# Batch 0 of a cosformer attention: k's sums by a selector weight, an earlier k^T v, and fewer idle matmuls

## The chip, the cores and the metric

The kernel runs on one core of a Trainium2 chip. The metric is the device time of one launch in microseconds (us). A core has five engines that run their own instruction queues in order and meet through semaphores: TensorE (matmuls and weight loads; PE and PEld in the profile), VectorE (DVE), ScalarE (ACT), GpSimd (POOL) and SyncE (SP), the last two also issuing DMAs. A matmul reads its two operands from SBUF and writes PSUM; VectorE and ScalarE carry PSUM back to SBUF.

## The reference

```python
def phi(x, c, s):                       # c, s: cos and sin of pi/2 * position / S
    r = np.maximum(x, 0.0)
    return np.concatenate([r * c, r * s], axis=-1)
q_p, k_p = phi(q, cos_w, sin_w), phi(k, cos_w, sin_w)
kv  = np.einsum('bhsf,bhsd->bhfd', k_p, v)
z   = np.sum(k_p, axis=2)
num = np.einsum('bhsf,bhfd->bhsd', q_p, kv)
den = np.einsum('bhsf,bhf->bhs', q_p, z)[..., None] + 1e-06
attn = num / den                        # 8 batches, 8 heads, S = 576, head size 64
x = attn.transpose(0, 2, 1, 3).reshape(B * S, H * D)          # 4608 x 512
h = x @ w_in                            # 512 -> 2048
g = h * (1.0 / (1.0 + np.exp(-1.702 * h)))
out = g @ w_out                         # 2048 -> 512
```

q, k, v, the weights and the output are float32; the matmuls run in bfloat16.

## The kernel before, in words

The sequence of a batch is cut into nine slots j of 64 rows. Two heads (hh) lie on the two halves of the 128 partitions, and four such pairs (i) side by side. For batch 0, k, q and v are loaded in this layout (`kf`, `qf0`, `vb`), k and q by SyncE in two pieces each (L62, L63), v as bfloat16 by GpSimd in two halves of two pairs (L130).

`trig` (L138 to L145) makes phi of one slot: two instructions, one with the cosine and one with the sine as a scale per partition, on VectorE or with `act=True` on ScalarE. It fills `kr` from k and `qn0` from q. `kv_mm` (L205 on) accumulates k^T v in PSUM for pairs i0 to i1 with `kr` as the stationary operand, a half of the partitions at a time; with a column of ones in place of v the same function gives k's sums, as column 64 beside the 64 of k^T v. `kv_evac` (L213) casts the result into `kvs`, from which later matmuls read 65 columns. `qturn_pe(c)` transposes q's slots 2c and 2c+1 on TensorE, `qevac(c)` carries them from PSUM into `qT`. `num_mm(c)` multiplies 128 rows of q with `kvs`, numerator and denominator in one (L223); `num_div(c)` divides on VectorE into `xn` (L231 to L235). `xturn_mm` (L253) and `xturn_evac` (L260, ScalarE) transpose xn into `xT`, which the first layer reads (`mm1_part`, L276). `start_block` interleaves the last of these with the first layer's first four column blocks of 128.

The order of work is written out by hand and each engine keeps it. PSUM tiles come from two pools: four buffers "mm" of one bank, two buffers "at" of two banks. `idle(n)` (L335) issues n matmuls of 512 columns on a tile of zeros, whose results nobody reads. The program starts with 23 of them, while k and q come in.

On GpSimd's queue stand, in this order: a small copy that waits for k's first piece (L128), v's halves for batch 0, two blocks of w_in (`load_win`, L122), a small copy that waits for v's second half (L133), the other two blocks of w_in, and then the loads of batch 1 and of w_out.

After batch 0's attention TensorE runs the two layers of one batch after the other, with the next batch's attention woven in; nothing of that is touched.

Of the kernel before, what the change touches and what calls it, by code (L numbers as in the profile page):

```python
# [9 lines left out]
F32 = mybir.dt.float32  # L10
BF16 = mybir.dt.bfloat16
AF = mybir.ActivationFunctionType
MUL = mybir.AluOpType.mult
ADD = mybir.AluOpType.add
MAX = mybir.AluOpType.max
# [4 lines left out]
def kernel(  # L20
# [9 lines left out]
    nc = tc.nc  # L30
# [5 lines left out]
    NS = S // 64  # L36
    MT = 512
    NI = H // 2

    const = ctx.enter_context(tc.tile_pool(name="const", bufs=1))  # L40
# [4 lines left out]
    small = ctx.enter_context(tc.tile_pool(name="small", bufs=3))  # L45
    pmm = ctx.enter_context(tc.tile_pool(name="pmm", bufs=4, space=PSUM))
# [5 lines left out]
    def raw(name, dt=F32):  # L52
        return one.tile([128, NI, S], dt, name=name)
# [5 lines left out]
    kf, vf, vb = raw("kf"), raw("vf"), raw("vb", BF16)  # L59
    qf0 = qf[:, 0:NI * S].rearrange("p (i e) -> p i e", i=NI)  # L60
    for t, src, cut in ((kf, k, 192), (qf0, q, 256)):
# [9 lines left out]
    ident = const.tile([128, 128], BF16)  # L71
# [3 lines left out]
    warm = const.tile([128, 512], BF16)  # L75
# [6 lines left out]
    scale = math.pi / 2.0 / S  # L82
    halfpi = const.tile([128, 1], F32)
    nc.vector.memset(halfpi, math.pi / 2.0)
    ones = const.tile([128, 2], BF16)
    nc.vector.memset(ones, 1.0)
    nc.scalar.activation(sinw, pos_f, AF.Sin, scale=scale)
    nc.scalar.activation(cosw, pos_f, AF.Sin, scale=-scale, bias=halfpi)
    gl = const.tile([128, 1], F32)
# [3 lines left out]
    kr = one.tile([128, NS, NI, 128], BF16, name="kr")  # L93
    vt = one.tile([128, NS, NI, VW], BF16, name="vt")
    qn = one.tile([128, 5, H, 128], BF16, name="qn")
    qn0 = qn.rearrange("p c h f -> p (c h f)")[:, 0:NS * NI * 128].rearrange(
        "p (j i f) -> p j i f", j=NS, i=NI)
# [23 lines left out]
    def load_win(g):  # L121
        nc.gpsimd.dma_start(out=w_in_sb[g], in_=win_r[:, :, ts(g, 512)])  # L122
# [4 lines left out]
    gate = const.tile([1, 4], F32)  # L127
# [2 lines left out]
        nc.gpsimd.dma_start(out=vb[:, i:i + 2], in_=src_of(v, 0, i, i + 2))  # L130
    load_win(0)
    load_win(1)
    nc.gpsimd.tensor_copy(gate[0:1, 1:2], vb[0:1, 3, 0:1])  # L133
    load_win(2)
    load_win(3)


    def trig(dst, src, j, act=False):  # L138
        i = src[:, :, ts(j, 64)]
        for cs, w in enumerate((cosw, sinw)):  # L140
            o = dst[:, j, :, ts(cs, 64)]
            if act:
                nc.scalar.activation(o, i, AF.Relu, scale=w[:, j:j + 1])
            else:
                nc.vector.tensor_scalar(o, i, 0.0, w[:, j:j + 1], op0=MAX, op1=MUL)  # L145

    def trig_q(c, act=False):
        n = 128 if c < 4 else 64
# [21 lines left out]
    def qturn_pe(c, home=None):  # L170
        tp = pmm.tile([128, 2, NI, 128], BF16, name="mm") if home is None else home
        for j in range(2 * c, min(2 * c + 2, NS)):
            for i in range(NI):
                nc.tensor.transpose(tp[:, j % 2, i], qn0[:, j, i, :], ident)  # L174
        tps[c] = tp

    def qevac(c, act=False):
        n = min(2 * c + 2, NS) - 2 * c
        o = qT[:, :, ds(c * 128, n * 64)].rearrange("f h (j p) -> f j h p", j=n)
        i = tps.pop(c)[:, 0:n].rearrange("f j i (hh p) -> f j (i hh) p", hh=2)  # L180
        if act:
            nc.scalar.activation(o, i, AF.Copy)
        else:
            nc.vector.tensor_copy(o, i)
# [10 lines left out]
    st = {}  # L195

    def kv_open(i0=0, i1=NI):
        t = pat.tile([128, 2, 512], F32, name="at")
        for i in range(i0, i1):
            st["kv", i] = t[:, :, ds((i - i0) * 65, 65)]  # L200
        st["ps", i0] = t[:, :, 0:(i1 - i0) * 65]
        if i0 == 0:
            st["kvs"] = small.tile([128, 2, NI, VW], BF16, name="kvs", bufs=2)

    def kv_mm(i0, i1, rhs, col, n):  # L205
        for i in range(i0, i1):
            for j in range(NS):
                for hh in range(2):
                    r = slice(hh * 64, hh * 64 + 64)
                    nc.tensor.matmul(st["kv", i][:, hh, ds(col, n)], kr[r, j, i, :], rhs(r, i, j),  # L210
                                     start=(j == 0), stop=(j == NS - 1))

    def kv_evac(i0, i1):  # L213
        o = st["kvs"][:, :, i0:i1, 0:65]
        nc.vector.tensor_copy(o, st["ps", i0].rearrange("p hh (i e) -> p hh i e", e=65))  # L215

    nums = {}

    def num_mm(c):
        ps = pat.tile([128, 2, 512], F32, name="at")  # L220
        for h in range(H):
            i, hh = divmod(h, 2)
            nc.tensor.matmul(ps[:, h // 4, ds((h % 4) * 65, 65)], qT[:, h, ts(c, 128)],  # L223
                             st["kvs"][:, hh, i, 0:65], start=True, stop=True)
        nums[c] = [ps]

    def num_div(c):
        ps = nums[c][0]
        pv = ps[:, :, 0:260].rearrange("p a (h e) -> p a h e", h=4)
        den = small.tile([128, 2, 4], F32, name="den")  # L230
        nc.vector.tensor_scalar(den, pv[:, :, :, 64], 1e-6, None, op0=ADD)  # L231
        inv = small.tile([128, 2, 4], F32, name="inv")
        nc.vector.reciprocal(inv, den)
        xn = small.tile([128, 2, 4, 64], BF16, name="xn", bufs=4)
        nc.vector.tensor_tensor(xn, pv[:, :, :, 0:64],  # L235
                                inv.unsqueeze(3).to_broadcast([128, 2, 4, 64]), op=MUL)
        nums[c].append(xn)
# [7 lines left out]
    def x_open(b):  # L245
        x[b] = xpool.tile([128, KC, S], BF16, name="xT")
# [85 lines left out]
                eng = nc.sync if b == B - 1 else nc.gpsimd  # L332
                eng.dma_start(out=dst[:, c0:c1], in_=ysb[p0:p0 + n, c0:c1])  # L333

    def idle(n, cols=512):  # L335
        w = pmm.tile([128, 512], F32, name="mm")
        for _ in range(n):
            nc.tensor.matmul(w[:, 0:cols], warm[:, 0:128], warm[:, 0:cols], start=True, stop=True)  # L338

    def vb_rhs(r, i, j):  # L340
        return vb[r, i, ts(j, 64)]
# [4 lines left out]
    def start_block(b, opened=False):  # L346

        if not opened:
            xturn_mm(0)
            xturn_evac(b, 0)  # L350
            num_mm(2)
            num_div(2)
            xturn_mm(1)
            xturn_evac(b, 1)
        for c in range(4):
            for fc in range(4):
                mm1_part(b, fc, c * 128, c * 128 + 128)
            if c == 0:
                num_mm(3)
                num_div(3)  # L360
                xturn_mm(2)
                xturn_evac(b, 2)
            if c == 1:
                num_mm(4)
                num_div(4)
                xturn_mm(3)
                xturn_evac(b, 3)
        for fc in range(4):
            gelu(fc)
        mm1(b, 4)  # L370
        xturn_mm(4)
        xturn_evac(b, 4)


    idle(23)
    for j in (0, 1):
        trig(kr, kf, j)
    for j in (2, 6, 7, 8):
        trig(kr, kf, j, act=True)
    for j in (3, 4, 5):  # L380
        trig(kr, kf, j)
    kv_open(0, 2)
    kv_open(2, 4)
    kv_mm(0, NI, lambda r, i, j: ones[r, 0:1], 64, 1)
    for j in (0, 1):
        trig(qn0, qf0, j)
    qturn_pe(0)
    for j in (2, 3):
        trig(qn0, qf0, j, act=True)
    qturn_pe(1)  # L390
    idle(3)
    for j in (4, 5):
        trig(qn0, qf0, j)
    qturn_pe(2)
    for j in (6, 7):
        trig(qn0, qf0, j, act=True)
    qevac(0)
    trig(qn0, qf0, 8)
    qevac(1)
    qevac(2, act=True)  # L400
    kv_mm(0, 2, vb_rhs, 0, 64)
    qturn_pe(3)
    qevac(3, act=True)
    kv_evac(0, 2)
    qturn_pe(4)
    qevac(4)
    kv_mm(2, 4, vb_rhs, 0, 64)
    kv_evac(2, 4)
    num_mm(0)
    num_div(0)  # L410
    num_mm(1)
    num_div(1)
    x_open(0)
    start_block(0)

# [44 lines left out]
    kv_open()  # L460
    kv_mm(0, 4, vt_rhs, 0, 65)
    kv_evac(0, 4)
    mm2(0, 2, 8, 12)
    mm2(0, 3, 8, 12)
# [96 lines left out]
```

## Time and profile before

| | us |
|---|---|
| three runs | 294.86, 296.48, 297.08 |
| median | 296.48 |
| the profiled execution's own time | 296.72 |
| its span, first to last instruction | 295.0 |
| TensorE busy | 288.4 (98%) |
| VectorE, ScalarE, GpSimd busy | 126.7, 130.7, 34.7 |

The span is what the rows of the profile cover; the time of the execution is a little longer. A row of the timeline gives start and duration of a run of like instructions, and in brackets how long the engine stood idle before it and what released it. Matmuls are pipelined, so the duration of one is longer than the distance to the next. The granted clock is the share of TensorE's full clock that its throttle let through. Over the whole span its mean is 0.994.

### The profile page before, as it was taken

How to read it: one execution, taken by the hardware profiler on the slowest of the kernel's cores; microseconds unless marked ns; L12 is line 12 of the kernel's file. 1: busy time of each engine (PE TensorE's matmuls, PEld its weight loads, DVE VectorE, ACT ScalarE, POOL GpSimd, SP SyncE). 2: the span in 40 equal slices, each digit the busy share in tenths (PEclk: the TensorE clock that was granted, in tenths of full speed). 3: DMA queues.
4: the chain of work that ended last, by engine and by line, in shares of the span. 5: the costliest groups of instructions: out<-in, count | busy, mean ns of one | idle time of the engine just before them, and what ended most of it. 6: DMA issues, size and time to landing. Idle time of an engine off the chain costs nothing.

```text
span 295.0 us, 6106 instructions
## 1 busy us (share of the span) xinstructions
PE 288.4 (98%) x2498; PEld 161.7 (55%) x2498; DVE 126.7 (43%) x363; ACT 130.7 (44%) x229; POOL 34.7 (12%) x68
## 2 busy tenths in 40 slices
PE   8979999999999999999999999999999999999995
PEld 2776656757454555455545554555455545565444
DVE  4855513693255825671567156454752420000000
ACT  7827653676014631374126412651166017773111
POOL 6340031500123001100110011000100010000000
PEclk9979999999999999999999999999999999999999
DMA  7999969667168974698569936996595240000321
GB/s 251 240 220 288 368 143 379 196 130 194 36 122 239 315 192 121 195 337 214 90 195 354 224 94 150 321 188 194 138 384 112 71 116 37 1 0 3 86 90 71
DMA packets 67227, 52.36 MB, mean 177 GB/s; under 512 B 47392, under 2 KB 57376, under 8 KB 67200
## 3 DMA queue, kind: packets, MB, share of 16 engines
q1 hardware_dynamic: 59824, 32.52, 42.8%
q0 software_dynamic: 7376, 19.47, 23.2%
q8 instruction: 19, 0.31, 0.4%
q14 instruction: 8, 0.07, 0.1%
HBM read 36.70 MB, written 9.44 MB: 156 GB/s over the span
## 4 chain that ended last, share of the span: by engine, by line
PE 98%; DVE 1%; ACT 0%; issue 0%; ACTq 0%
PE mm L326 42%; PE mm L276 38%; PE at L210 4%; PE mm L294 4%; PE at L223 3%; PE mm L338 3%; PE mm L303 1%; PE at L253 1%; PE mm L174 1%; PE at L174 1%; DVE xn L235 0%; ACT xT L260 0%; DVE kvs L215 0%; ACT ysb L330 0%; DVE warm L76 0%
## 5 line engine op out<-in xcount | busy, mean ns | idle before, releaser
L326 PE MATMUL mm<-w_out_sb,g 128*128 128x512 bf16 (+1 forms) x528 | 117.7, 373 | 0.0
L276 PE MATMUL mm<-xT,w_in 128*128 128x512 bf16 (+1 forms) x608 | 114.4, 348 | 0.0
L281 ACT ACTIVATE g<-mm 128x512 bf16<-128x512 f32 x128 | 75.6, 598 | 31.9 <-PE mm L276 31.9
L276 PEld LDWEIGHTS <-w_in 128*128 128x128 bf16 x608 | 62.7, 115 | 49.0
L326 PEld LDWEIGHTS <-g 128*128 128x128 bf16 x528 | 48.7, 98 | 49.5
L330 ACT ACTIVATE ysb<-mm 128x512 f32<-128x512 f32 (+1 forms) x37 | 21.7, 586 | 111.4 <-PE mm L326 111.4
L333 POOL DMA_DIRECT2D out_dram<-ysb x38 | 20.7, 548 | 177.3 <-ACT ysb L330 177.2
L145 DVE TENSOR_SCALAR kr<-kf,cosw 128x256 bf16<-128x256 f32 x68 | 23.6, 348 | 27.8 <-DMA kf<-in_k_dram 27.8
L235 DVE TENSOR_TENSOR xn<-at,inv 128x512 bf16<-128x512 f32 x40 | 27.6, 691 | 1.4
L145 DVE TENSOR_SCALAR kr<-kf,sinw 128x256 bf16<-128x256 f32 x68 | 23.8, 350 | 0.0
L231 DVE TENSOR_SCALAR den<-at 128x8 f32<-128x8 f32 x40 | 6.6, 166 | 38.6 <-PE at L223 38.6
L223 PEld LDWEIGHTS <-qT 128*128 128x128 bf16 x320 | 15.0, 99 | 8.6 <-issue 1.2
L215 DVE CAST kvs<-at 128x520 bf16<-128x520 f32 (+1 forms) x9 | 5.8, 642 | 29.8 <-PE at L210 29.8
L223 PE MATMUL at<-kvs,qT 128*128 128x65 bf16 x320 | 16.5, 195 | 1.0 <-ACT xT L260 0.7
L158 DVE TENSOR_SCALAR qn<-qf,sinw 128x512 bf16<-128x512 f32 (+1 forms) x30 | 14.3, 477 | 0.0
L158 DVE TENSOR_SCALAR qn<-qf,cosw 128x512 bf16<-128x512 f32 (+1 forms) x30 | 14.3, 477 | 0.0
L210 PEld LDWEIGHTS <-kr 64*128 64x128 bf16 x648 | 10.2, 94 | 2.8 <-issue 2.0
L294 PE MATMUL mm<-xt,w_in 128*128 128x384 bf16 x64 | 10.6, 326 | 0.0
L326 PE MATMUL mm<-w_out_sb,gl_t 128*128 128x512 bf16 x48 | 10.5, 379 | 0.0
L338 PE MATMUL mm<-warm 128*128 128x512 bf16 x26 | 8.6, 502 | 1.3 <-DVE warm L76 1.3
L294 PEld LDWEIGHTS <-w_in 128*128 128x128 bf16 x64 | 7.2, 113 | 3.3
L260 ACT ACTIVATE xT<-at 128x512 bf16<-128x512 bf16 (+1 forms) x10 | 5.6, 562 | 7.7 <-PE at L253 6.6
(60 smaller groups left out, 123.5 us busy)
## 6 DMA issues: line engine op xcount, KB each, us to landing
kf<-in_k_dram SPq DMA_DIRECT2D x5, 1152.0 KB, 6.7
vf<-in_v_dram SPq DMA_DIRECT2D x5, 1152.0 KB, 9.5
qf<-in_q_dram SPq DMA_DIRECT2D x5, 1024.0 KB, 6.2
out_dram<-ysb POOLq DMA_DIRECT2D x20, 256.0 KB, 3.1
kf<-in_k_dram POOLq DMA_DIRECT2D x2, 1152.0 KB, 10.2
vf<-in_v_dram POOLq DMA_DIRECT2D x2, 1152.0 KB, 14.8
out_dram<-ysb POOLq DMA_DIRECT2D x18, 128.0 KB, 2.7
w_in<-in_moe_w_in_dram POOLq DMA_DIRECT2D x4, 512.0 KB, 10.0
```

The source lines that it names most:

```text
L145: nc.vector.tensor_scalar(o, i, 0.0, w[:, j:j + 1], op0=MAX, op1=MUL)
L158: nc.vector.tensor_scalar(o, i, 0.0, sc, op0=MAX, op1=MUL)
L210: nc.tensor.matmul(st["kv", i][:, hh, ds(col, n)], kr[r, j, i, :], rhs(r, i, j), start=(j == 0), stop=(j == NS - 1))
L223: nc.tensor.matmul(ps[:, h // 4, ds((h % 4) * 65, 65)], qT[:, h, ts(c, 128)], st["kvs"][:, hh, i, 0:65], start=True, stop=True)
L235: nc.vector.tensor_tensor(xn, pv[:, :, :, 0:64], inv.unsqueeze(3).to_broadcast([128, 2, 4, 64]), op=MUL)
L276: nc.tensor.matmul(hp[fc][:, t0:t1], w_in_of(kc, fc), x[b][:, kc, t0:t1], start=(kc == 0), stop=(kc == KC - 1))
L281: nc.scalar.activation(g, hp.pop(fc), AF.Gelu_apprx_sigmoid)
L294: nc.tensor.matmul(hps, w_in_of(kc, fc), xt[:, kc, :], start=(kc == 0), stop=(kc == KC - 1))
L326: nc.tensor.matmul(yp[t, c0][:, c0:c1], w, w_out_sb[:, fc, c0:c1], start=(fc == 0), stop=(fc == FC - 1))
L330: nc.scalar.activation(ysb[:, c0:c1], yp[t, c0][:, c0:c1], AF.Identity)
L333: eng.dma_start(out=dst[:, c0:c1], in_=ysb[p0:p0 + n, c0:c1])
L338: nc.tensor.matmul(w[:, 0:cols], warm[:, 0:128], warm[:, 0:cols], start=True, stop=True)
```

## The change

All of it is in batch 0, ahead of the first layer's first matmul.

- The ones become a selector `sel` of two columns: column hh is 1 on head hh's half of the partitions and 0 elsewhere. `ksum(j)` takes it as the stationary operand and a whole slot of `kr` (512 columns) as the moving one, so nine matmuls replace 72 and give the sums as two rows of 512 in a "mm" buffer. VectorE copies these rows to SBUF (`zr`), `ksum_turn` turns them back with four small transposes, and VectorE puts them into column 64 of `kvs`. `kv_evac` of batch 0 now takes 64 columns.
- The leading idle matmuls are 12 instead of 23. One stands ahead of the ninth sum, one ahead of q's first transposes, and two instead of three behind these. Four more stand between `num_mm(1)` and the first transposes of x. `idle` can go on in a buffer that it has.
- q's slot 8 is rotated on GpSimd instead of VectorE, between w_in's second block and the copy that waits for v.
- The first half of k^T v now stands right behind the transposes of the sums and ahead of q's slots 6 and 7; the second half comes ahead of slot 8's transposes instead of behind them. The evacuation of slots 2 and 3 follows on VectorE behind that of the sums, and slot 8's evacuation goes to ScalarE.

```diff
-    ones = const.tile([128, 2], BF16)
-    nc.vector.memset(ones, 1.0)
+    sel = const.tile([128, 2], BF16)
+    nc.vector.memset(sel, 0.0)
+    for hh in range(2):
+        nc.vector.memset(sel[hh * 64:hh * 64 + 64, hh:hh + 1], 1.0)
...
     load_win(0)
     load_win(1)
-    nc.gpsimd.tensor_copy(gate[0:1, 1:2], vb[0:1, 3, 0:1])
-    load_win(2)
-    load_win(3)
...
+    def ksum(j):
+        if j == 0:
+            st["z"] = pmm.tile([128, 512], F32, name="mm")
+        nc.tensor.matmul(st["z"][0:2], sel, kr[:, j].rearrange("p i f -> p (i f)"),
+                         start=(j == 0), stop=(j == NS - 1))
+
+    def ksum_turn():
+        zt = pmm.tile([128, NI, 2], BF16, name="mm")
+        for i in range(NI):
+            nc.tensor.transpose(zt[:, i], st["zr"][:, ts(i, 128)], ident[0:2, 0:2])
+        nc.vector.tensor_copy(st["kvs"][:, :, :, 64], zt.rearrange("f i hh -> f hh i"))
...
-    idle(23)
+    w = idle(12)
...
     kv_open(0, 2)
     kv_open(2, 4)
-    kv_mm(0, NI, lambda r, i, j: ones[r, 0:1], 64, 1)
+    for j in (0, 1, 2, 3, 6, 4, 7, 5):
+        ksum(j)
+    idle(1, w)
+    ksum(8)
     for j in (0, 1):
         trig(qn0, qf0, j)
+    st["zr"] = small.tile([2, 512], BF16, name="zr", bufs=1)
+    nc.vector.tensor_copy(st["zr"], st["z"][0:2])
+    idle(1, w)
     qturn_pe(0)
     for j in (2, 3):
         trig(qn0, qf0, j, act=True)
+    idle(2, w)
     qturn_pe(1)
-    idle(3)
     for j in (4, 5):
         trig(qn0, qf0, j)
+    trig(qn0, qf0, 8, eng=nc.gpsimd)
+    nc.gpsimd.tensor_copy(gate[0:1, 1:2], vb[0:1, 3, 0:1])
+    load_win(2)
+    load_win(3)
     qturn_pe(2)
     for j in (6, 7):
         trig(qn0, qf0, j, act=True)
     qevac(0)
-    trig(qn0, qf0, 8)
-    qevac(1)
+    ksum_turn()
     qevac(2, act=True)
     kv_mm(0, 2, vb_rhs, 0, 64)
+    qevac(1)
+    kv_evac(0, 2, 64)
     qturn_pe(3)
     qevac(3, act=True)
-    kv_evac(0, 2)
+    kv_mm(2, 4, vb_rhs, 0, 64)
+    kv_evac(2, 4, 64)
     qturn_pe(4)
-    qevac(4)
-    kv_mm(2, 4, vb_rhs, 0, 64)
-    kv_evac(2, 4)
+    qevac(4, act=True)
     num_mm(0)
     num_div(0)
     num_mm(1)
     num_div(1)
+    idle(4)
     x_open(0)
     start_block(0)
```

More of the change, by code (lines that the diff above doesn't have):

```diff
@@ L132, with trig @@
     load_win(1)
-    nc.gpsimd.tensor_copy(gate[0:1, 1:2], vb[0:1, 3, 0:1])
-    load_win(2)
-    load_win(3)
-    def trig(dst, src, j, act=False):
+    def trig(dst, src, j, act=False, eng=nc.vector):
         i = src[:, :, ts(j, 64)]
@@ L144, in trig @@
             else:
-                nc.vector.tensor_scalar(o, i, 0.0, w[:, j:j + 1], op0=MAX, op1=MUL)
+                eng.tensor_scalar(o, i, 0.0, w[:, j:j + 1], op0=MAX, op1=MUL)
     def trig_q(c, act=False):
@@ L211, in kv_mm, with kv_evac @@
                                      start=(j == 0), stop=(j == NS - 1))
-    def kv_evac(i0, i1):
-        o = st["kvs"][:, :, i0:i1, 0:65]
-        nc.vector.tensor_copy(o, st["ps", i0].rearrange("p hh (i e) -> p hh i e", e=65))
+    def kv_evac(i0, i1, n=65):
+        o = st["kvs"][:, :, i0:i1, 0:n]
+        nc.vector.tensor_copy(o, st["ps", i0].rearrange("p hh (i e) -> p hh i e", e=65)[:, :, :, 0:n])
+    def ksum(j):
[8 more added lines that the diff above has]
+        nc.vector.tensor_copy(st["kvs"][:, :, :, 64], zt.rearrange("f i hh -> f hh i"))
     nums = {}
@@ L333, in mm2, with idle @@
                 eng.dma_start(out=dst[:, c0:c1], in_=ysb[p0:p0 + n, c0:c1])
-    def idle(n, cols=512):
-        w = pmm.tile([128, 512], F32, name="mm")
+    def idle(n, w=None):
+        if w is None:
+            w = pmm.tile([128, 512], F32, name="mm")
         for _ in range(n):
-            nc.tensor.matmul(w[:, 0:cols], warm[:, 0:128], warm[:, 0:cols], start=True, stop=True)
+            nc.tensor.matmul(w, warm[:, 0:128], warm, start=True, stop=True)
+        return w
     def vb_rhs(r, i, j):
```

## The prediction

> **What bounds the kernel now.** I read the page's shares first, then the two big matmul groups, then TensorE's timeline.
>
> ```profile
> PE 288.4 (98%) x2498; PEld 161.7 (55%) x2498; DVE 126.7 (43%) x363; ACT 130.7 (44%) x229; POOL 34.7 (12%) x68
> ...
> L326 PE MATMUL mm<-w_out_sb,g 128*128 128x512 bf16 (+1 forms) x528 | 117.7, 373 | 0.0
> L276 PE MATMUL mm<-xT,w_in 128*128 128x512 bf16 (+1 forms) x608 | 114.4, 348 | 0.0
> ```
>
> TensorE is busy in 98% of the span, and its two large groups stood idle for 0.0 us. What comes after batch 0's attention therefore cannot shrink; it can only begin earlier. The edits all lie ahead of it, so the question is when the dense stream begins. Here is TensorE up to that point (start, duration, what; where rows overlap I take start to start):
>
> ```profile
> 1.26 7.84 PE L338 MATMUL mm<-warm 128*128 128x512 bf16 x23 [1.26 <-DVE warm L76]
> 9.03 1.05 PE L210 MATMUL at<-ones,kr 64*128 64x1 bf16 x72
> 10.01 1.07 PE L174 MATMUL mm<-ident,qn 128*128 128x128 bf16 x16
> 10.91 0.81 PE L338 MATMUL mm<-warm 128*128 128x512 bf16 x3
> 11.56 0.61 PE L174 MATMUL mm<-ident,qn 128*128 128x128 bf16 x8
> 12.11 0.71 PE L210 MATMUL at<-vb,kr 64*128 64x64 bf16 x36
> 12.74 0.84 PE L174 MATMUL mm<-ident,qn 128*128 128x128 bf16 x12
> 13.52 0.71 PE L210 MATMUL at<-vb,kr 64*128 64x64 bf16 x36
> ...
> 14.75 0.52 PE L223 MATMUL at<-kvs,qT 128*128 128x65 bf16 x12 [0.30 <-DVE kvs L215]
> 16.26 0.40 PE L253 MATMUL at<-ident,xn 128*128 128x128 bf16 x4 [0.98 <-DVE xn L235]
> 17.34 0.60 PE L223 MATMUL at<-kvs,qT 128*128 128x65 bf16 x8 [0.69 <-ACT xT L260]
> ...
> 18.16 1.91 PE L276 MATMUL mm<-xT,w_in 128*128 128x128 bf16 x16
> 19.87 0.65 PE L223 MATMUL at<-kvs,qT 128*128 128x65 bf16 x8
> ...
> 20.58 1.06 PE L276 MATMUL mm<-xT,w_in 128*128 128x128 bf16 x16
> 21.48 0.41 PE L223 MATMUL at<-kvs,qT 128*128 128x65 bf16 x8
> ...
> 21.97 2.99 PE L276 MATMUL mm<-xT,w_in 128*128 128x128 bf16 x36
> ```
>
> The 21.97 row, where the third column block of the first layer starts, is my marker: whatever moves it moves the end. Two marks stand ahead of it. N, 14.75, is the second half of num_mm(0), released by the cast of k^T v. S, 17.34, is num_mm(2), released by the first xT copy. S follows N by 2.59 us through VectorE, TensorE and ScalarE, whose own speed the edits leave alone.
>
> One more thing lies between S and the marker: the same 16 narrow matmuls last 1.71 us from 18.16 (to 19.87) and 0.90 us from 20.58 (to 21.48). The stages, cut where the clock changes, say why (columns: window, its length, busy us of PE, PEld, DVE, ACT, POOL with counts, granted clock, DMA):
>
> ```profile
> 6.76:10.17 3.41, 3.41 (x86) 2.01 (x85) 3.08 (x12) 3.41 (x10) 0.79 (x2) 1.00 1.14 313
> 10.17:13.58 3.41, 3.41 (x79) 2.80 (x79) 2.74 (x8) 2.88 (x7) 1.50 (x3) 1.00 1.24 210
> 13.58:17.00 3.42, 1.79 (x57) 1.40 (x57) 2.65 (x8) 1.15 (x2) 3.42 (x6) 1.00 1.23 203
> 17.00:20.41 3.41, 3.07 (x37) 3.07 (x37) 1.30 (x4) 0.89 (x2) 0.62 (x2) 0.50 1.24 208
> 20.41:23.82 3.41, 3.41 (x66) 3.41 (x64) 2.12 (x6) 1.73 (x4) 0.55 (x1) 1.00 1.14 338
> ```
>
> After a stretch in which TensorE was busy for 1.79 of 3.42 us, the granted clock is 0.50 for the next 3.41 us. The idle matmuls show the clock's other change (the ones of the first 5 us, then those after 7 us):
>
> ```profile
> L338 PE MATMUL mm<-warm 128*128 128x512 bf16 x12 | 5.3, 629 | 1.3 <-DVE warm L76 1.3
> ...
> L338 PE MATMUL mm<-warm 128*128 128x512 bf16 x10 | 2.3, 379 | 0.0
> ```
>
> **The change, part by part.** The rows for the other engines:
>
> ```profile
> 8.16 0.49 ACT L143 ACTIVATE kr<-kf,sinw 128x256 bf16<-128x256 f32 x1
> ...
> 8.90 0.34 DVE L145 TENSOR_SCALAR qn<-qf,sinw 128x256 bf16<-128x256 f32 x1
> 9.57 0.35 DVE L145 TENSOR_SCALAR qn<-qf,cosw 128x256 bf16<-128x256 f32 x1 [0.33 <-DMA qf<-in_q_dram]
> ...
> 10.36 0.34 DVE L145 TENSOR_SCALAR qn<-qf,sinw 128x256 bf16<-128x256 f32 x1
> ...
> 14.27 0.43 DVE L215 CAST kvs<-at 128x260 bf16<-128x260 f32 x1 [0.22 <-PE at L210]
> ...
> 15.51 0.69 DVE L235 TENSOR_TENSOR xn<-at,inv 128x512 bf16<-128x512 f32 x1
> ```
> ```profile
> 1.44 0.29 POOL L73 TENSOR_SCALAR_AFFINE_SELECT ident<-ident 128x128 bf16<-128x128 bf16 x1
> ...
> 1.77 0.53 POOL L102 MEMSET qT<- 128x512 bf16 x1
> ...
> 12.08 0.18 POOL L133 CAST gate<-vb 1x1 f32<-1x1 bf16 x1 [4.54 <-DMA vb<-in_v_dram]
> ```
>
> *k's sums and the leading idle matmuls.* Twelve idle matmuls at 0.427 us (23 less those at full clock, 7.84 us in all) end near 6.4. Nine selector matmuls of 512 columns follow, at about 0.22 us each (the 16 narrow ones give 0.056 per 128 columns), each as its slot of k is ready; the last slot is ready at 8.16 + 0.49 = 8.65. The sums are ready near 9.1, where the 72 one-column matmuls began at 9.03 and ran to 10.01. That frees 0.98 us of TensorE, and the three idle matmuls after it (0.65 us) become three in places where TensorE waits anyway.
>
> What is late next is q's rotation on VectorE. The copy of the sums (2x512 from PSUM; nearest row the 128x512 at 15.51, 0.61 to the next start) enters at 9.17, behind the op at 8.90. The op that DMA held to 9.57 then starts at 9.78, 0.21 late, so slot 5's sine ends at 10.36 + 0.21 + 0.34 = 10.91 instead of 10.70. Transposes start at 10.97.
>
> *From there TensorE is in line.* Slot 5's four transposes 0.27 (half of 11.56 to 12.11); four transposes of the sums, at most as wide, 0.2 (bounds 0.1 to 0.27): 11.44. First half of k^T v 0.63 (12.11 to 12.74): 12.07. Eight transposes of q 0.55: 12.62. Second half to its cast 0.75 (13.52 to 14.27): 13.37. The cast to N 0.48 (14.27 to 14.75): **N = 13.85, 0.90 earlier.** Data in time: v's second half had landed by the gate's 12.08, against 12.62; the first half was issued ahead of it. On VectorE the sums' evacuation, q's second evacuation and the first half's cast fit between 11.6 and 13.0. Slot 8's transposes (four, 0.26) lie inside the wait for the cast. Their evacuation goes to ScalarE, whose next use is the xT copy at N + 1.9.
>
> *Slot 8 on GpSimd.* No row has this operation there. Nearest by elements per partition are the two rows above (128 and 512: 0.29 and 0.53); I take 0.4 each, 0.8 for both, ready by 10.4 with q's landing at 9.57. From below it is worth up to the 0.53 us of VectorE that it frees, but that lies behind slot 5 and does not reach N; from above the pair costs nothing until about 13.2, when slot 8 is transposed. The gate and the loads of w_in behind it on GpSimd's queue waited for v until 12.08 anyway. A fight over ports with VectorE's four ops from 9.78 could lengthen these: beside DMA issues on GpSimd this form ran 0.59 at most (below) against 0.34. Two such ops put N at +0.5; none is the nearer to most rows.
>
> ```profile
> L145 DVE TENSOR_SCALAR kr<-kf,sinw x14: 334/344/595, 4.6 to 30.6; 128x256 bf16<-128x256 f32 x14
> ```
>
> *Four idle matmuls ahead of the first x transposes.* 4 x 0.22 = 0.86 us, from N + 0.40 to N + 1.26; the transposes need xn at N + 1.51. At full clock they cost nothing, at half clock (0.427 each, 1.71) they end at N + 2.1 to 2.3 and delay S by 0.6 to 0.8. Their stretch, 13.58 to 17.0, then has idle time only of 0.06 + 0.12 + 0.68 us, so 2.5 of 3.42 us busy against 1.79. I expect the clock to stay at 1.00. No row shows a stretch between 1.79 and 3.07, so the threshold is open.
>
> *Sum at full clock.* S = 13.85 + 2.59 = 16.44. From S to the marker by the full-clock rows: num_mm(2) and transposes 0.49 (21.48 to 21.97), 16 narrow 0.90, then 0.49, 0.90, 0.49: 3.27 instead of 4.63. xn(2) and xn(3) arrive just ahead of their transposes (0.44 + 0.43 + 0.70 = 1.57 after num_mm against 1.65 of other TensorE work). The marker falls to 19.71: 0.90 + 1.36 = **2.26 us earlier**. w_in's first load lies between 5.99 and 18.4 and was no wait at 18.16; it is needed at 16.9, and a later load that reuses its queue slot went out at 16.25 without waiting.
>
> ```profile
> 16.25 0.81 POOL L113 DMA_DIRECT2D vf<-in_v_dram x1
> ```
>
> The profiled execution took 296.72 us (span 295.0 plus 1.7), 0.24 above the median of 296.48 and inside the 294.86 to 297.08 shown. 296.72 - 2.26 = 294.46; I say **294.5**. A change of 1%, 2.96 us, is about what a measurement of this kernel can tell from none.
>
> **Rivals.**
>
> *A: the clock falls all the same.* Then 0.50 holds from 17.00 to 20.41. S at 16.44, transposes to 16.93, 16 narrow 1.71 to 18.64, 0.71 (19.87 to 20.58) to 19.35, 1.06 of the next 1.71 until 20.41, the remaining 38% at full clock 0.34, then 0.49: 21.24. Gain 0.73, **296.0**. For it: 2.5 of 3.42 is no full stretch. Against: the idle matmuls stream without a pause.
>
> *B: the clock falls a stretch earlier, and the change is a loss of little or nothing.* Ahead of N the new order has almost only transposes and half-height matmuls after 9.2. If 10.17 to 13.58 counts as idle, the four idle matmuls run at half clock from about N + 0.6 and S comes at 17.2, with half clock to 20.41: gain 0.1, **296.6**. Against it: that stretch before had 20 transposes, 72 halves and three idle matmuls, and it was followed by 1.00. The Trainium skill (TensorE: Matmul & The Clock Gate, Part 4: PE-mode transpose) says that transposes do not count as TensorE being busy in the same way, which would favour this case; the 1.00 row for 13.58 to 17.00 speaks against it, though three full matmuls helped there.
>
> *C, slower: slot 8 comes late from GpSimd.* TensorE takes its transposes in order, ahead of num_mm(0), and N waits. It decides from a pair of ops that lasts beyond 13.2 - 9.6 = 3.6 us; the gain is used up at 3.6 + 2.26 = 5.9 us, 2.9 us an op, against 0.29 to 0.53 in the rows. At 6.8 us (0.8 of work and a start of 6) it gives 296.72 + 0.9 = **297.6**. The Trainium skill (GPSIMD Engine Reference, section 2.1, Instruction dispatch) states about 6 us for the first call of a freshly loaded GpSimd kernel, which is where such a start would come from; the short GpSimd rows at 1.44 and 1.77 show none for their first calls.
>
> *D: ports.* GpSimd slows VectorE: N 0.5 later, gain 1.8, **295.0**; also the case that parts of my chain are 0.5 too short.
>
> **How the numbers follow.** Forecast 45%, A 22%, B 10%, C with any other loss 10%, D 13%. Around the forecast I allow 0.9 us below: the bounds of the sums' transposes (0.1), the copy of the sums hidden (0.2), and the spread of the runs, half of 2.2 us, in part; this gives 293.4. Above, the range takes in A, B and D and ends at 297.2, inside C. Faster by over 1% (below 293.5) needs 2.97 us below the median, more than any case: 9%. Slower by over 1% (above 299.4) needs C with a pair of 8.8 us, or a fault not seen: 6%. The rest, 85%, is within 1%.
>
> **What the new profile would show.** Right: the selector matmuls end near 9.1; N at 13.7 to 14.0; granted clock 1.00 from 6.8 on without a break; the idle four end before xn; the third block of 128-column matmuls at 19.5 to 20.0; the rest of the span unchanged. Wrong: 0.50 in any stretch after 7 us (A, B), TensorE waiting on GpSimd's slot 8 (C), VectorE's q ops above 0.40 us (D), or a new wait in the matmul stream, which would break the step from marker to end.

## The result, and the profile after

| | runs | median us | lowest to highest |
|---|---|---|---|
| before | 22 | 295.10 | 294.86 to 297.08 |
| changed | 22 | 294.63 | 294.47 to 294.96 |

The ratio of the runs is 0.9963, with a 95% interval of 0.9949 to 0.9976: a small gain, clear of noise and far below the 1% that the forecast had taken for what can be told from none. The forecast time was 294.5, which is 2.0 less than the median of the three runs known then; the medians of 22 lie only 0.47 apart.

The median hides something that the three runs shown before did not tell. The 22 runs of before lie in two groups, twelve from 294.86 to 295.11 (median 295.0) and ten from 296.39 to 297.08 (median 296.56), with nothing between. The changed kernel has one group. So the change is worth 0.4 us against one part of the old executions and 1.9 us against the other. The profile on which the prediction was built was one of the upper group.

The profiled execution of the changed kernel took 294.68 us (span 293.0), 2.04 less than that of before; the sum had said 2.26. Here is TensorE's timeline of the changed kernel, in the columns used above. L348 are idle matmuls, L217 the selector, L171 q's transposes, L223 the sums' transposes, L207 k^T v, L232 num_mm, L262 x's transposes, L285 the first layer:

```profile
8.67 0.39 PE L348 MATMUL mm<-warm 128*128 128x512 bf16 x1
8.99 0.38 PE L217 MATMUL mm<-kr,sel 128*2 128x512 bf16 x1
...
10.40 1.18 PE L171 MATMUL mm<-ident,qn 128*128 128x128 bf16 x16
11.52 0.25 PE L223 MATMUL mm<-ident,zr 2*128 2x2 bf16 x4
11.70 0.71 PE L207 MATMUL at<-vb,kr 64*128 64x64 bf16 x36
12.34 0.62 PE L171 MATMUL mm<-ident,qn 128*128 128x128 bf16 x8
12.89 0.71 PE L207 MATMUL at<-vb,kr 64*128 64x64 bf16 x36
13.53 0.40 PE L171 MATMUL mm<-ident,qn 128*128 128x128 bf16 x4
13.76 0.88 PE L232 MATMUL at<-kvs,qT 128*128 128x65 bf16 x16
14.48 1.02 PE L348 MATMUL mm<-warm 128*128 128x512 bf16 x4
15.62 0.40 PE L262 MATMUL at<-ident,xn 128*128 128x128 bf16 x4
16.71 0.40 PE L232 MATMUL at<-kvs,qT 128*128 128x65 bf16 x8 [0.69 <-ACT xT L269]
...
17.17 1.06 PE L285 MATMUL mm<-xT,w_in 128*128 128x128 bf16 x16
18.06 0.41 PE L232 MATMUL at<-kvs,qT 128*128 128x65 bf16 x8
...
19.93 2.99 PE L285 MATMUL mm<-xT,w_in 128*128 128x128 bf16 x36
```

The marker stands at 19.93 instead of 21.97, and those 2.04 us are the whole difference: the rest of the span only begins earlier. S is at 16.71, and the way from S to the marker takes 3.22 us instead of 4.63. The first 16 narrow matmuls now take 0.89 us (17.17 to 18.06), as the second 16 did before. N is hidden in the row at 13.76; the chain of the same execution shows it as the second half of num_mm(0), behind the cast (start, duration, what):

```profile
13.64 0.44 DVE kvs L212
...
14.12 0.29 PE at L232 x4
```

The stages, cut at the clock's own steps of 3.41 us as this execution had them (columns as above, the granted clock third from the end):

```profile
5.63:9.04 3.41, 3.06 (x13) 0.73 (x11) 2.88 (x11) 2.76 (x7) 2.05 (x3) 1.00 1.10 371
9.04:12.46 3.42, 3.42 (x71) 2.54 (x71) 3.30 (x10) 3.42 (x9) 2.63 (x2) 1.00 1.21 206
12.46:15.87 3.41, 3.22 (x72) 2.24 (x71) 2.20 (x8) 1.98 (x3) 3.41 (x6) 1.00 1.25 210
15.87:19.28 3.41, 2.72 (x56) 2.60 (x54) 2.46 (x8) 1.71 (x3) 2.98 (x5) 1.00 1.23 203
```

No stage has the 0.50 that stood at 17.00 to 20.41. GpSimd and VectorE hold the surprise, first GpSimd's timeline, then VectorE's:

```profile
9.82 2.33 POOL L142 TENSOR_SCALAR qn<-qf,cosw 128x256 bf16<-128x256 f32 x1 [2.14 <-DMA qf<-in_q_dram]
12.15 1.13 POOL L142 TENSOR_SCALAR qn<-qf,sinw 128x256 bf16<-128x256 f32 x1
13.25 0.18 POOL L412 CAST gate<-vb 1x1 f32<-1x1 bf16 x1
```
```profile
9.40 0.68 DVE L402 CAST zr<-mm 2x512 bf16<-2x512 f32 x1
10.01 0.33 DVE L142 TENSOR_SCALAR qn<-qf,cosw 128x256 bf16<-128x256 f32 x1
...
10.80 0.34 DVE L142 TENSOR_SCALAR qn<-qf,sinw 128x256 bf16<-128x256 f32 x1
11.06 0.67 DVE L181 COPY qT<-mm 128x1024 bf16<-128x1024 bf16 x1
```

Slot 8 on GpSimd took 3.46 us instead of the 0.8 forecast. It was ready at 13.28, and its transposes stand at 13.53: a quarter of a microsecond was left.

### The profile page after: what moved, and what is told of

Read it like the earlier page. It is cut to its first block, busy times and chain, and to the rows that moved or that the text cites. A ratio compares the mean times of both kernels' runs of the same rounds, so it can differ in the third digit from the quotient of the medians.

```text
span 293.0 us, 5983 instructions
## 1 busy us (share of the span) xinstructions
PE 287.1 (98%) x2433; PEld 159.3 (54%) x2433; DVE 126.5 (43%) x364; ACT 131.1 (45%) x230; POOL 38.2 (13%) x70
## 4 chain that ended last, share of the span: by engine, by line
PE 95%; DMA 2%; DVE 1%; ACT 0%; issue 0%; SPq 0%; ACTq 0%
PE mm L335 43%; PE mm L285 38%; PE mm L303 4%; PE at L207 3%; PE at L232 3%; DMA kf<-in_k_dram 2%; PE mm L312 1%; PE at L262 1%; PE mm L171 1%; PE at L171 1%; DVE kr L142 1%; PE mm L217 0%; PE mm L348 0%; DVE xn L244 0%; ACT xT L269 0%
## 5 line engine op out<-in xcount | busy, mean ns | idle before, releaser
L285 PE MATMUL mm<-xT,w_in 128*128 128x512 bf16 (+1 forms) x608 | 113.5, 345 | 0.0
L285 PEld LDWEIGHTS <-w_in 128*128 128x128 bf16 x608 | 61.9, 114 | 49.0
L232 PEld LDWEIGHTS <-qT 128*128 128x128 bf16 x320 | 14.6, 97 | 8.3 <-issue 1.0
L232 PE MATMUL at<-kvs,qT 128*128 128x65 bf16 x320 | 16.1, 193 | 0.8 <-ACT xT L269 0.7
L207 PEld LDWEIGHTS <-kr 64*128 64x128 bf16 x576 | 9.2, 94 | 2.3 <-issue 2.0
L303 PEld LDWEIGHTS <-w_in 128*128 128x128 bf16 x64 | 7.2, 113 | 3.3
L304 ACT ACTIVATE gl_t<-mm 128x384 bf16<-128x384 f32 x16 | 7.8, 490 | 2.4 <-PE mm L303 2.4
L163 DVE CAST vt<-vf 128x2304 bf16<-128x2304 f32 (+1 forms) x7 | 8.9, 1265 | 0.0
```

What stands on the lines that cost most here:

```text
L285: nc.tensor.matmul(hp[fc][:, t0:t1], w_in_of(kc, fc), x[b][:, kc, t0:t1], start=(kc == 0), stop=(kc == KC - 1))
L303: nc.tensor.matmul(hps, w_in_of(kc, fc), xt[:, kc, :], start=(kc == 0), stop=(kc == KC - 1))
```

## The experiments

Two questions had to be settled: which edit takes away the upper group, and what sets N. Each run's result has its mean granted clock over the span, and it tells the groups apart: of 35 further runs of before on the chip of the first two experiments below, 18 at 294.94 to 295.69 had 0.998 to 1.000, and 17 at 296.37 to 297.05 had 0.993 or 0.994. Half a clock for 3.41 of 295 us makes 0.994: an upper run is one with one stage at 0.50. How many runs are upper ones differs from set to set: 10 of the first 22, 17 of these 35, and 10 of 35, 6 of 23 and 3 of 15 on three other chips.

### Without the four idle matmuls behind N

```diff
     num_div(1)
-    idle(4)
     x_open(0)
```

> The changed kernel without the four idle matmuls ahead of x's first transposes. The runs of before lie in two groups, 294.9 to 295.1 and 296.4 to 297.1. Theory: the upper group are executions in which the granted clock falls to 0.50 after the thin stretch behind N, and the four idle matmuls fill that stretch; without them N stays at 14.1, S at 16.7, and the runs split again, some at 294.6, some 1.4 to 1.5 us higher near 296.1, those with a mean clock of about 0.994. Rival: the two groups come from the first rise of the clock under the 23 leading idle matmuls, and the shorter lead removed them; then all runs stay within 0.3 us of 294.6.

Of twelve runs ten came to 294.46 to 294.91 with a clock of 0.998 or more, and two to 296.13 and 296.24 with 0.993. The theory holds in kind: the upper runs are back, 1.5 to 1.7 us above the rest. The frequency is lower, 2 in 12 against 17 in 35 of before on this chip, though twelve runs are too few to call that a difference. In the profiled execution, one of the ten, the stage behind N was busy for 2.12 us and the clock stayed, where 1.79 us had let it fall:

```profile
14.94:18.36 3.42, 2.12 (x42) 2.00 (x43) 2.59 (x7) 1.20 (x2) 3.30 (x5) 1.00 1.24 208
18.36:21.77 3.41, 3.41 (x66) 3.35 (x64) 2.12 (x6) 1.79 (x4) 1.10 (x2) 1.00 1.26 220
```

The clock changes at steps of 3.41 us that do not start with the kernel: the rise came at 6.76 us in the profile of before and at 4.00 in that of the next experiment, whose instructions are the same up to N; in the changed kernel it came at 5.63, and at 5.40 when that kernel was profiled again. So where a step's edge falls into the thin stretch differs from run to run.

### The kernel before, with only the four idle matmuls

```diff
     num_div(1)
+    idle(4)
     x_open(0)
```

> The kernel before with nothing added but the four idle matmuls at the same place. Theory: the upper group vanishes and all runs come near 295.0, the lower group of before, so that what is left to the changed kernel, 0.4 us, is the earlier N. Rival (first rise of the clock): both groups stay, at 295.0 and 296.5.

Ten of twelve runs came to 295.01 to 295.52, all with 1.000 or 0.998, and two stayed at 296.51 and 296.61 with 0.993. Against 17 in 35 of before on this chip that is fewer, but with twelve runs again not surely so, and the upper group has not vanished. One of the two was profiled, and its fall is at another place, while the fill behind N works:

```profile
7.41:10.83 3.42, 2.79 (x91) 2.15 (x91) 3.20 (x12) 3.42 (x10) 0.18 (x1) 1.00 1.17 273
10.83:14.24 3.41, 3.41 (x52) 2.57 (x52) 1.97 (x5) 2.08 (x4) 2.12 (x4) 0.50 1.23 206
14.24:17.65 3.41, 2.94 (x68) 2.01 (x68) 2.13 (x7) 1.02 (x1) 2.86 (x5) 1.00 1.24 206
```

TensorE's rows show what filled the stage that cost the clock:

```profile
7.66 0.29 PE L210 MATMUL at<-ones,kr 64*128 64x1 bf16 x10
...
8.75 0.85 PE L210 MATMUL at<-ones,kr 64*128 64x1 bf16 x56 [0.24 <-ACT kr L143]
9.54 1.21 PE L174 MATMUL mm<-ident,qn 128*128 128x128 bf16 x16
```

By the records that stage was busy for 2.79 of 3.42 us, more than the 2.12 that kept the clock above. It was busy with one-column matmuls and with transposes. So the selector, too, may serve the clock; the next run takes it away.

### The selector undone

```diff
...
-    w = idle(12)
+    idle(21)
...
-    for j in (0, 1, 2, 3, 6, 4, 7, 5):
-        ksum(j)
-    idle(1, w)
-    ksum(8)
+    kv_mm(0, NI, lambda r, i, j: ones[r, 0:1], 64, 1)
...
-    st["zr"] = small.tile([2, 512], BF16, name="zr", bufs=1)
-    nc.vector.tensor_copy(st["zr"], st["z"][0:2])
-    idle(1, w)
...
-    idle(2, w)
...
-    ksum_turn()
```

The casts of k^T v take 65 columns again.

> The changed kernel with k's sums made the old way, 72 one-column matmuls on kr, behind 21 leading idle matmuls; the rows' copy, the sums' transposes and the three idle matmuls among q's transposes go with the selector, all else stays. Theory 1: without the copy on VectorE slot 5 of q ends 0.3 earlier, and N is set by TensorE in line at about 13.8, so an execution at full clock takes 294.3. Theory 2: the one-column matmuls and the transposes behind them count little as activity; the profile of before with four idle matmuls added showed 0.50 from 10.8 to 14.2 behind just that stretch. Then a part of the runs (some 2 in 12) takes about 1.4 us more, at a mean clock of 0.993, though the four idle matmuls are in place. Rival: those runs came from chance or from the missing fill behind N alone; then no run leaves 294.2 to 294.8.

Nine of twelve runs took 294.27 to 294.65 (median 294.47), 0.16 below the changed kernel, which was not run on this chip. At full clock the old sums are thus no slower, as far as these runs tell, than the selector with its copy, its transposes and its idle matmuls. Three runs took 295.62, 295.73 and 297.03 with 0.994; the last is 2.6 us above the nine, more than one stage at half clock can cost (1.7), and what else it lost is not shown. The profiled one, at 295.62, shows the fall behind the one-column matmuls and q's transposes:

```profile
7.80:11.22 3.42, 2.83 (x88) 2.32 (x88) 3.29 (x11) 3.42 (x10) 1.63 (x2) 1.00 1.19 256
11.22:14.63 3.41, 3.41 (x85) 2.89 (x83) 1.36 (x4) 2.60 (x4) 3.22 (x6) 0.50 1.23 205
```

What the selector buys is then not the 0.98 us of TensorE; it is that 512-column matmuls stand where one-column ones let the clock fall. In part this is argued, because this run also leaves out the idle matmuls among q's transposes. The last kernel below leaves those out too and keeps the selector, and none of its eleven runs fell, on a chip where 3 in 15 of before did.

The changed kernel's 22 runs, and the 12 of its repetition (below), have no mean clock under 0.998. It has both fills, the selector and the four idle matmuls. The three kernels with one of them have 2, 2 and 3 in 12. On the same two chips the four other kernels with both fills and no new wait of TensorE for GpSimd (the next two experiments and the first two tries of the last) had none in 46 runs, where before had 17 in 35 and 10 in 35. So both fills together keep the clock; what one alone is worth stays open, since 3 in 12 is no fewer than the 10 in 35 of before on that chip.

### 23 leading idle matmuls

```diff
-    w = idle(12)
+    w = idle(23)
```

> The changed kernel with 23 leading idle matmuls instead of 12, nothing else. They end between 7.7 and 9.1, depending on when the clock rises, and the nine selector matmuls then run back to back for 1.94 us; the sums are ready at 10.0 to 11.4 instead of 9.4, and VectorE, which takes the rows' copy ahead of q's slots 4 and 5, is held as long. Theory: N 0.6 to 2.0 later, time 295.2 to 296.6, spread over the runs. Rival: TensorE has room in this stretch and the lead does not matter; then 294.6 to 294.8.

Measured 296.44 (ten runs, 295.40 to 297.00, all at full clock). VectorE's rows show the mechanism:

```profile
8.94 0.34 DVE L142 TENSOR_SCALAR qn<-qf,sinw 128x256 bf16<-128x256 f32 x1
11.22 0.68 DVE L402 CAST zr<-mm 2x512 bf16<-2x512 f32 x1 [1.94 <-PE mm L217]
```

The rows' copy stands in VectorE's queue ahead of q's slots 4 and 5 and waits 1.94 us for the sums; q waits with it. The shorter lead is a part of the selector, not a saving of its own.

### Slot 8 on VectorE

```diff
-    trig(qn0, qf0, 8, eng=nc.gpsimd)
...
     qevac(0)
+    trig(qn0, qf0, 8)
     ksum_turn()
```

> The changed kernel with q's slot 8 rotated on VectorE again, behind the evacuation of slots 0 and 1; GpSimd's pair took 2.33 and 1.13 us in the changed kernel. Theory: neither place is on the path to N; VectorE has 0.74 us free ahead of the second cast, the pair there takes 0.53, so the time stays at 294.6, within 0.1, and GpSimd's copy that waits for v goes back from 13.3 to about 12.2. Rival: VectorE is what sets N, then N and the time come 0.3 to 0.5 later.

Measured 294.74 (twelve runs, 294.52 to 294.97), against 294.63 and, in its repetition, 294.72 for the changed kernel. The move to GpSimd is worth nothing that these runs can tell.

### Slot 8 twice on GpSimd

```diff
-    trig(qn0, qf0, 8, eng=nc.gpsimd)
+    for _ in range(2):
+        trig(qn0, qf0, 8, eng=nc.gpsimd)
```

> The changed kernel with GpSimd's rotation of slot 8 done twice in a row (four ops). In the changed kernel the pair took from 9.82 to 13.28, against transposes at 13.53. Theory of the third rival: beyond that point each us of GpSimd is a us of the whole. If ops 3 and 4 take 1.13 each like the second one, the four end near 15.6, N comes 2.0 later and the time is 296.5 (up to 298 if the clock falls in the wait). If the first op's 2.33 was a start-up paid once, this is the same; if it was VectorE's four q ops holding the port, also; the first op alone does not tell these apart here. Rival: slot 8 is not on the path; then 294.6.

Six of ten runs took 296.06 to 296.62 at full clock, 1.8 above the changed kernel, and four 297.29 to 297.71 with 0.993 or 0.994, though both fills are in place. TensorE's longer wait is what is new; where those four fell is not shown, since the profiled execution kept its clock. GpSimd's rows, then TensorE's:

```profile
9.64 2.63 POOL L142 TENSOR_SCALAR qn<-qf,cosw 128x256 bf16<-128x256 f32 x1 [1.84 <-DMA qf<-in_q_dram]
12.28 1.13 POOL L142 TENSOR_SCALAR qn<-qf,sinw 128x256 bf16<-128x256 f32 x1
...
14.52 1.13 POOL L142 TENSOR_SCALAR qn<-qf,sinw 128x256 bf16<-128x256 f32 x1
```
```profile
15.71 0.40 PE L171 MATMUL mm<-ident,qn 128*128 128x128 bf16 x4 [1.99 <-POOL qn L142]
```

The third rival's mechanism is real and priced about right: beyond 13.5 a microsecond of GpSimd is about one of the whole. Slot 8's transposes came 2.18 us later than in the changed kernel, and the profiled execution took 1.94 more.

Why the first op takes 2.33 or 2.63 is seen across the runs. In the kernel with 23 leading idle matmuls VectorE was waiting when GpSimd began, and the first op took no longer than the others:

```profile
9.68 1.14 POOL L142 TENSOR_SCALAR qn<-qf,cosw 128x256 bf16<-128x256 f32 x1 [2.07 <-ACT qn L140]
```

So there is no start-up. In the changed kernel VectorE's four q ops ran beside the first op, from 10.01 to 11.06, at their usual 0.33, and GpSimd lost 1.2 us; its repetition has the same 2.33. In two later kernels it was VectorE's ops that took longer (below). The rows show that the two engines get in each other's way. By what, and what decides which of them pays, these runs leave open.

### The rows' copy later, three tries

The copy held q's slots 4 and 5. The first try puts it behind them, and the sums' transposes behind the first half of k^T v.

```diff
     for j in (0, 1):
         trig(qn0, qf0, j)
-    st["zr"] = small.tile([2, 512], BF16, name="zr", bufs=1)
-    nc.vector.tensor_copy(st["zr"], st["z"][0:2])
     idle(1, w)
...
+    st["zr"] = small.tile([2, 512], BF16, name="zr", bufs=1)
+    nc.vector.tensor_copy(st["zr"], st["z"][0:2])
     qevac(0)
-    ksum_turn()
     qevac(2, act=True)
     kv_mm(0, 2, vb_rhs, 0, 64)
     qevac(1)
+    ksum_turn()
```

> The changed kernel with the copy of the sums' rows on VectorE moved behind q's slots 4 and 5, and the sums' transposes moved behind the first half of k^T v. Theory: the copy held slots 4 and 5 back by some 0.35 us and with them everything to N, and the sums' transposes another 0.18 of it; slot 5 then ends near 10.8, N near 13.8, and the time falls by 0.3 to 294.3. Rival: N is set by ScalarE's slots 6 and 7 (ready at 11.97) or by v's landing; then N stays at 14.1 and the time at 294.6.

Measured 295.34, 0.7 slower than the changed kernel and neither as the theory nor as the rival had it. TensorE's rows name the cause:

```profile
10.24 0.61 PE L171 MATMUL mm<-ident,qn 128*128 128x128 bf16 x8
11.48 0.61 PE L171 MATMUL mm<-ident,qn 128*128 128x128 bf16 x8 [0.63 <-DVE zr L417]
```

Slots 4 and 5 get the PSUM buffer of the sums, which the copy frees only at 11.43. The second try gives them the idle matmuls' buffer:

```diff
-    qturn_pe(2)
+    qturn_pe(2, w.bitcast(BF16).rearrange("p (j i f) -> p j i f", j=2, i=NI))
```

> The changed kernel with the rows' copy behind q's slots 4 and 5 and the sums' transposes behind the first half of k^T v, as in the run that came out at 295.3; there the transposes of slots 4 and 5 waited for that copy until 11.48, because their PSUM buffer was the one of the sums. Here they get the idle matmuls' buffer by name. Theory: the buffer alone made that run slow; now slots 4 and 5 are turned by 11.2, N is near 13.8 and the time 294.3, 0.3 below the changed kernel. Rival: something else of the order (the copies on VectorE) holds N; then 294.6 or more.

Measured 294.69 (294.55 to 295.22): the buffer was the loss, but the gain did not come, and the rival was right. GpSimd and VectorE began within 0.2 us of each other, GpSimd's first op took 1.20, and of VectorE's four ops two took longer, as they had in the first try:

```profile
9.58 0.35 DVE L142 TENSOR_SCALAR qn<-qf,cosw 128x256 bf16<-128x256 f32 x1 [0.34 <-DMA qf<-in_q_dram]
9.85 0.57 DVE L142 TENSOR_SCALAR qn<-qf,sinw 128x256 bf16<-128x256 f32 x1
10.34 0.34 DVE L142 TENSOR_SCALAR qn<-qf,cosw 128x256 bf16<-128x256 f32 x1
10.60 0.49 DVE L142 TENSOR_SCALAR qn<-qf,sinw 128x256 bf16<-128x256 f32 x1
```

The third try moves slot 8 to ScalarE, behind slots 6 and 7; it was run beside the changed kernel itself.

```diff
-    trig(qn0, qf0, 8, eng=nc.gpsimd)
...
-    for j in (6, 7):
+    for j in (6, 7, 8):
         trig(qn0, qf0, j, act=True)
```

> The last order (the rows' copy behind q's slots 4 and 5, the sums' transposes behind the first half of k^T v, the idle matmuls' buffer for slots 4 and 5) with slot 8 rotated on ScalarE behind slots 6 and 7, so that GpSimd does nothing beside VectorE's q ops. In that order GpSimd's first op took 1.20 and two of VectorE's four q ops grew to 0.57 and 0.49, and slot 5 ended at 11.1, no earlier than in the changed kernel. Theory: the port, not TensorE's line, ate the gain of the later copy; without GpSimd slot 5 ends at 10.75, N comes near 13.8 and the time is 294.3, 0.3 below the changed kernel on the same chip. Rival: TensorE's line or ScalarE's later slots (two ops more, 0.8) hold N at 14.1; then 294.6 or more.

> The changed kernel itself, unaltered, as the measure for the other kernel of this pair: 294.5 to 295.0, no run with a mean clock below 0.998.

Measured 294.76 against 294.72 for the changed kernel on the same chip. Slot 5 was ready at 10.63, as expected, but TensorE was not there: it stood in line, with four idle matmuls and the selector's last ones between 8.46 and 11.0. The second eight of these sixteen transposes are slots 4 and 5:

```profile
10.28 0.35 DVE L142 TENSOR_SCALAR qn<-qf,sinw 128x256 bf16<-128x256 f32 x1
```
```profile
10.51 1.06 PE L171 MATMUL mm<-ident,qn 128*128 128x128 bf16 x16
```

The rival held again, and it named the next step:

```diff
-    idle(1, w)
     qturn_pe(0)
...
-    idle(2, w)
     qturn_pe(1)
```

> The last order again (slot 8 on ScalarE, the rows' copy late) without the idle matmul ahead of q's first transposes and the two behind them. In that run slot 5 of q was ready at 10.62, but TensorE had stood in line without a gap since 8.46 and reached slot 5's transposes only at about 11.0. Theory: with q earlier, these three idle matmuls (about 0.75 us with their weight loads) are on the path; without them TensorE waits for slot 3 (ScalarE, 10.3), N comes near 13.75 and an execution at full clock takes 294.3 to 294.4. A part of the runs may show a mean clock of 0.994 and 1 to 1.5 us more, if the three were needed as activity. Rival: N stays at 14.1, the time at 294.7.

Measured 294.43 (eleven runs, 294.23 to 294.66), the fastest kernel of this study; its ratio to before on its chip is 0.9967 (0.9952 to 0.9983). No run had a clock under 0.998. TensorE waits where it should, N came at 13.69 where 13.75 was expected, and the marker is at 19.50, 0.43 earlier than in the changed kernel:

```profile
10.32 0.84 PE L171 MATMUL mm<-ident,qn 128*128 128x128 bf16 x12 [0.28 <-ACT qn L140]
...
19.50 1.00 PE L285 MATMUL mm<-xT,w_in 128*128 128x128 bf16 x15
```

The profiled execution is the fastest of the eleven. The medians of the two kernels lie 0.2 to 0.3 apart, and they were not run side by side.

## Why the prediction was right, and where it was not

**The bound** held: everything behind the marker moved as a block, 2.04 us in the span's profile and 2.04 in time.

**N** came at 14.12, not 13.85, and outside the 13.7 to 14.0 that was named. The step that failed is the copy of the sums "at 9.17, behind the op at 8.90": it started at 9.40, because the sums were ready at 9.37 and not "near 9.1". Of the difference 0.11 is k's landing, later in this execution (VectorE's first op at 4.41 against 4.30), and the rest, about 0.1, is the idle matmul ahead of the last sum, 0.32 from start to start (8.67 to 8.99) where I had 0.22. The chain behind it was right to a few hundredths: 0.18 for the sums' transposes (0.2), 0.64, 0.55 and 0.75 as worked out.

**N as a gain** was measured against one execution. Before's own N depends on when the clock rises: with the rise at 4.00 instead of 6.76 its one-column matmuls began at 7.66 and were done at 9.6 instead of 10.08. That may be why the lower group is only 0.37 above the changed kernel, and not 0.63; no profile of the lower group was taken. Side by side on one chip, the lower group lay at 295.04 and the full-clock runs of the changed kernel without its four idle matmuls at 294.59, 0.45 apart.

**From S to the marker** 3.27 was forecast, 3.22 measured, and N to S came out at 2.59 exactly. The four idle matmuls ended at 15.50, ahead of the transposes at 15.62, as forecast.

**The clock** was the larger term, 1.36 us, and the experiments confirm it: runs of low mean clock are 0.9 to 1.7 us longer than the others of their kernel, one 2.6. What the forecast lacked is that the fall comes in some executions only, 46 of 130 of before over all five sets, and that it had a second place. This is the step that failed for the gain: 2.26 was taken off an execution of the upper group as if all had the fall. The time came right all the same, because the changed kernel has one group and the sum led from that execution to it. The second rival expected the fall ahead of N in the *changed* kernel; the runs showed it with the *old* sums, behind the one-column matmuls. The page that it named, the Trainium skill (TensorE: Matmul & The Clock Gate, Part 4: PE-mode transpose), agrees with that fall in so far as transposes filled a part of that stage; no run here separates them from the one-column matmuls, and the changed kernel kept 1.00 behind a stage with 24 transposes in it.

**The first rival** did not come, but its price for the fall, 296.0, was good: without the four idle matmuls two runs took 296.13 and 296.24.

**The third rival** was nearer than its chance. The step at fault is the size of slot 8 on GpSimd, "0.4 each, 0.8 for both": an op takes 1.14 alone, and the first took 2.33 beside VectorE. The nearest rows, a memset and a select, write without reading float32 from SBUF at this width. That it cost nothing was luck: 3.46 was just under the 3.6 from which it decides, and no row had bounded the size of the op. Slot 8 twice then cost 1.8, where 1.9 was expected. The start of about 6 us that the Trainium skill states for the first call of a freshly loaded GpSimd kernel (GPSIMD Engine Reference, section 2.1, Instruction dispatch) did not appear: the first op took 1.14 where VectorE was out of the way.

**The fourth rival** was on the mark in that the two engines got in each other's way, and pointed the wrong way: VectorE's ops kept 0.33 us, and GpSimd paid. That a port is the cause is not shown.

## What to carry to other kernels

Look at all runs before a profile is priced: where they lie in two groups, find which group the profile belongs to, and count a term that only that group has at its share. Fill thin stretches with matmuls of many columns where the granted clock can fall, and judge the fill by the clock over many runs, since a single profile shows only one of the possible places. An idle matmul is free only as long as the work behind it is late: when q was made earlier here, the fill was the next thing on the path.

## What the runs showed of the hardware that was not expected

- The granted clock changes in steps of 3.41 us. The first edges fell at 4.00, 4.39, 4.70, 5.63 and 6.76 us of five profiles. Busy time in the records does not tell whether a step keeps it: 2.79 and 2.83 of 3.42 us, full of one-column matmuls and transposes, lost it, while 2.12 us of other work kept it.
- A rotation of 128x256 from float32 to bfloat16 takes 0.34 us on VectorE (0.27 to the next start) and 1.13 to 1.14 on GpSimd with VectorE's q ops out of the way. Side by side one of them takes longer: GpSimd's op grew to 2.33 and 2.63 in two kernels, two of VectorE's to 0.49 and 0.57 in two others.
- GpSimd sent w_in's last two blocks 1.2 us later than before (13.38 against 12.21) with no trace in TensorE's line.
